# Grouped-query attention over a cache: PV three batches behind QK, K loads five ahead of V, and wo issued by GpSimd in sixteen pieces

## The chip, the core and the metric

The kernel runs on one core of a Trainium2 chip. The metric is device time in microseconds: the median of several executions. Beside it stands a profile of one execution, whose span is the time from the first to the last instruction that the profiler saw on the core.

The engines: TensorE (PE; its weight loads are shown apart as PEld), VectorE (DVE), ScalarE (ACT), GpSimd (POOL) and SyncE (SP), which here issues all DMAs. PE writes to PSUM, which has eight banks; DVE and ACT copy from there to SBUF.

## The reference

```python
B, Sq, D = 32, 4, 1024
Hq, Hkv, Sk, Dh = 32, 4, 2048, 128
q = (x @ wq).reshape(B, Sq, Hq, Dh)                  # heads to the front
k, v = k_cache, v_cache                              # each KV head serves 8 query heads
scores = einsum("bhqd,bhkd->bhqk", q, k) * Dh ** -0.5
p = softmax(scores)
o = einsum("bhqk,bhkd->bhqd", p, v)
out = o.reshape(B, Sq, Hq * Dh) @ wo
```

All is bf16. The K and V caches are 67 MB each, wq and wo 8.4 MB each. For each batch there are 4 KV heads, and 8 query heads x 4 queries = 32 rows of scores to each, so 128 rows in all, over 2048 keys.

## The kernel before

**The helper.** `Program` (L13) holds one list of operations for each engine. Each operation names the events it waits for and may name an event that it sets; `emit` (L39) turns these into semaphore waits. The order of each list is written out by hand and is the order on that engine. DMAs are in the list of the engine that issues them.

**The stream of loads** (L121 to L165). All large loads go through nine slots of SBUF (`NSLOT`), 2 MB each, in a fixed order: four loads of wq, then K of batches 0, 1, 2, then V0, K3, V1, K4 and so on (K three ahead of V), at the end V29, V30, V31, and four loads of wo, the last of which is cut in four DMAs of 512 KB. Load number n goes to slot n mod 9, so it waits until what load n - 9 brought has been used (`freed`, L131): for K that is the last transpose of the batch, for V its PV. SP issues them all. A load of K or V is 128 partitions x 4 heads x 4 KB runs; wo has runs of 2 KB. In this text a load's place is its number in the stream, counted from 0.

**The start.** x is transposed on PE (L201) and multiplied with wq into eight PSUM banks (L209); DVE and ACT copy q, transposed, to `QT_sb`.

**The loop over batches** (PE's order: L299 to L311). K has keys on partitions and must have the head dimension there, so PE transposes it: eight fills (`kt_fill`, L232) of eight transposes each, into four ring banks in turn, from which DVE (five) and ACT (three) copy to `KT_sb` (`evac`, L339). This is done two batches ahead (`AHEAD`). In iteration i PE does

- `qk(i)` (L281): 16 matmuls give the scores of 128 rows x 2048 keys, in four PSUM banks,
- `pv(i - 1)` (L262): 64 matmuls, V stationary, P^T moving, into the fourth ring bank (`ps_o`),
- the eight fills of K for batch i + 2,
- `tr_fill` (L249) x4: P is transposed by 16 matmuls against a diagonal matrix that holds 1/sum, so it is normalized by the way; two copies by DVE and two by ACT bring it to `PT_sb`, of which there is one.

Between QK and the transposes of P stand DVE's maximum over the scores (L379), its scaled negative (L380), ACT's exponential with the row sums (L408), and DVE's reciprocal (L388) and diagonal (L389). `ot_evac` (L365) copies the result of PV to `oT_sb`, for all heads and batches.

**The end.** After the loop come `pv(31)` and the output projection (`oproj`, L313): for each of 32 heads two matmuls of 512 columns, accumulated over all heads in two banks. It waits for wo and for the last `ot_evac`. DVE and ACT copy half of the result each (L398, L418), and SP stores it (L166).

**What ties the ring together.** `ring_waits` (L183) makes a fill wait for the copy out of what was in its bank four fills ago, and for the fourth bank also for the `ot_evac` of the PV that used it in between.

Of the kernel before, what the change touches and what calls it, by code (L numbers as in the profile page):

```python
# [6 lines left out]
ALU = mybir.AluOpType  # L7
# [47 lines left out]
def bass_standalone__gqa_block_cached__sampling_kernel(  # L55
# [17 lines left out]
    G = Hkv  # L73
    scale = float(Dh) ** -0.5
    NSLOT = 9
    SLOT = 8192
    NRING = 4
    KT_FILLS = 2 * G
    TR_FILLS = 4
    AHEAD = 2  # L80
    WQ_LOADS = 4
    WO_LOADS = 4
    HPL = Hq // WO_LOADS

# [5 lines left out]
    with ExitStack() as es:  # L90
# [5 lines left out]
        pp_sb = sb("pp_sb", [128, 2, Sk], BF16)  # L96
# [6 lines left out]
        P_sb = pp_sb[:, 0, :]  # L103
        PT_sb = pp_sb[:, 1, :].rearrange("p (t r) -> p t r", r=128)
        x_sb = pp_sb[:, 0, 0:D]
        xT_sb = pp_sb[:, 0, D:2 * D].rearrange("p (a b) -> p a b", b=128)
        out_sb = pp_sb[:, 1, 0:D]
# [9 lines left out]
        for n in ["x", "out"] + [f"slot{i}" for i in range(NSLOT)] + [f"wo{i}" for i in range(4)]:  # L117
            pr.sems[n] = es.enter_context(nc.semaphore(f"s_{n}"))
# [3 lines left out]
        for b in range(AHEAD + 1):  # L122
            stream.append(("k", b))
        for b in range(B):
            stream.append(("v", b))
            if b + AHEAD + 1 < B:
                stream.append(("k", b + AHEAD + 1))
# [7 lines left out]
        def slot(l):  # L135
            return slots[:, slot_of[l], :]
# [4 lines left out]
        pr.load("sp", lambda e: e.dma_start(x_sb, x_flat[:, :]), "x", "x", 16)  # L141
        for n, l in enumerate(stream):
            kind, i = l
            waits = [freed(stream[n - NSLOT])] if n >= NSLOT else []
            s, v = f"slot{n % NSLOT}", 16 * (n // NSLOT + 1)
            if kind == "wq":
                fn = lambda e, l=l, i=i: e.dma_start(slot(l), wq_v[:, i, :])  # L147
            elif kind in "kv":
                src = (k_cache if kind == "k" else v_cache)[i].rearrange("g (p t) d -> p g (t d)", p=128)
                fn = lambda e, l=l, src=src: e.dma_start(slot(l).rearrange("p (g f) -> p g f", g=G), src)  # L150
            if kind != "wo":
                pr.load("sp", fn, l, s, v, waits)
                continue
            last = i == WO_LOADS - 1
            parts = 4 if last else 1
            per = HPL // parts
            for q in range(parts):
                fn = lambda e, l=l, i=i, q=q, per=per: e.dma_start(
                    slot(l)[:, q * per * D:(q + 1) * per * D].rearrange("p (h n) -> p h n", n=D),
                    wo_v[:, i * HPL + q * per:i * HPL + (q + 1) * per, :],  # L160
                )
                if last:
                    pr.load("sp", fn, ("wo", i, q), f"wo{q}", 16, waits)
                else:
                    pr.load("sp", fn, l, s, v, waits)  # L165
# [4 lines left out]
        jobs = [("kt", b, f) for b in range(AHEAD) for f in range(KT_FILLS)]  # L170
        for i in range(B):
            if i + AHEAD < B:
                jobs += [("kt", i + AHEAD, f) for f in range(KT_FILLS)]
            jobs += [("tr", i, f) for f in range(TR_FILLS)]
        job_index = {j: n for n, j in enumerate(jobs)}
# [6 lines left out]

        def ring_waits(job):  # L183
            n = job_index[job]
            if n < NRING:
                return [("q_evac", n)]
            w = [("evac",) + jobs[n - NRING]]
            if n % NRING == 3:
                b = job[1] - AHEAD - 1 if job[0] == "kt" else job[1] - 1
                if b >= 0:  # L190
                    w.append(("ot", b))
            return w


        pr.op("pool", lambda e: e.memset(ident[:], 0.0), [], "zero")
        pr.op("pool", lambda e: e.affine_select(
            out=ident[:], in_=ident[:], compare_op=ALU.not_equal, fill=1.0, base=0,
            pattern=[[-1, 128]], channel_multiplier=1), ["zero"], "ident")
# [33 lines left out]
        def kt_fill(b, f):  # L232
            job = ("kt", b, f)
            dst = ring_bf16[job_index[job] % NRING]
            g, half = f // 2, f % 2

            def fn(e):
                for q in range(8):
                    t = half * 8 + q
                    ins = e.transpose(  # L240
                        dst[:, q * 128:(q + 1) * 128],
                        slot(("k", b))[:, (g * NKT + t) * Dh:(g * NKT + t + 1) * Dh],
                        ident[:, :],
                    )
                return ins

            pr.op("pe", fn, [("k", b)] + ring_waits(job), job)

        def tr_fill(b, f):  # L249
            job = ("tr", b, f)  # L250
            dst = ring_f32[job_index[job] % NRING]

            def fn(e):
                for q in range(4):
                    t = f * 4 + q
                    ins = e.matmul(dst[:, q * 128:(q + 1) * 128], lhsT=P_sb[:, t * 128:(t + 1) * 128],  # L256
                                   rhs=diag[:, b % 2, :], start=True, stop=True)
                return ins

            pr.op("pe", fn, [("exp", b), ("diag", b)] + ring_waits(job), job)  # L260

        def pv(b):  # L262
            def fn(e):
                v = slot(("v", b))
                for g in range(G):
                    for t in range(NKT):
                        ins = e.matmul(  # L267
                            ps_o[:, 32 * g:32 * (g + 1)],
                            lhsT=v[:, (g * NKT + t) * Dh:(g * NKT + t + 1) * Dh],
                            rhs=PT_sb[:, t, 32 * g:32 * (g + 1)],  # L270
                            start=(t == 0),
                            stop=(t == NKT - 1),
                        )
                return ins

            w = [("v", b)] + [("evac", "tr", b, f) for f in range(TR_FILLS)]
            if b > 0:
                w.append(("ot", b - 1))
            pr.op("pe", fn, w, ("pv", b))

        def qk(i):  # L281
            def fn(e):
                for c in range(Sk // 512):
                    for g in range(G):
                        ins = e.matmul(  # L285
                            ps_s[32 * g:32 * (g + 1), c * 512:(c + 1) * 512],
                            lhsT=QT_sb[:, i, REP * g:REP * (g + 1), :],
                            rhs=KT_sb[:, i % 2, g, c * 512:(c + 1) * 512],
                            start=True,
                            stop=True,  # L290
                            tile_position=(0, 32 * g),
                        )
                return ins

            w = [("evac", "kt", i, f) for f in range(KT_FILLS)]
            w += [("q_evac", j) for j in range(NB)] if i == 0 else [("exp", i - 1)]
            pr.op("pe", fn, w, ("qk", i))
# [4 lines left out]
        for i in range(B):  # L302
            qk(i)
            if i >= 1:
                pv(i - 1)
            if i + AHEAD < B:
                for f in range(KT_FILLS):
                    kt_fill(i + AHEAD, f)
            for f in range(TR_FILLS):
                tr_fill(i, f)  # L310
        pv(B - 1)  # L311

        def oproj(i, h0, n, name):  # L313
# [15 lines left out]
        for i in range(WO_LOADS):  # L329
            last = i == WO_LOADS - 1  # L330
            parts = 4 if last else 1
            for q in range(parts):
                n = HPL // parts
                pr.op("pe", oproj(i, i * HPL + q * n, n, None),
                      [("wo", i, q) if last else ("wo", i), ("ot", B - 1), ("exp", B - 1)],
                      "oproj" if last and q == parts - 1 else None)


        def evac(job):  # L339
            eng = consumer(job)  # L340
            kind, b, f = job
            n = job_index[job]
            if kind == "kt":
                g, half = f // 2, f % 2
                src = ring_bf16[n % NRING]
                dst = KT_sb[:, b % 2, g, half * 1024:(half + 1) * 1024]
                w = [job] + ([("qk", b - 2)] if b >= 2 else [])
            else:
                src = ring_f32[n % NRING]
                dst = PT_sb[:, 4 * f:4 * f + 4, :].rearrange("p a b -> p (a b)")  # L350
                w = [job] + ([("pv", b - 1)] if b > 0 else [])
# [26 lines left out]
        for i in range(B):  # L378
# [3 lines left out]
            if i >= 1:  # L382
                ot_evac(i - 1)
# [13 lines left out]
        ot_evac(B - 1)  # L397
# [73 lines left out]
```

## Time and profile before

| what | value |
|---|---|
| median of 3 runs | 388.87 us (388.68 to 389.89) |
| the profiled execution's own time | 388.88 us |
| its span | 386.9 us |
| PE, DVE, ACT busy | 77%, 63%, 51% of the span |
| GpSimd busy | 0.7 us |
| bytes read | 151.26 MB |
| mean granted TensorE clock | 0.938 |
| output projection | 64 matmuls from 368.45 to 383.32 us |

The profile's page has six parts: busy time of each engine; the span in 40 slices of 9.67 us, each digit a busy share in tenths, with the granted TensorE clock, the DMA engines' share and GB/s; DMA queues; the chain of work that ended last; groups of instructions; and DMA issues with their time to landing. Beside the page, the trace can be asked for the instructions in order of time, for who waited for whom, and for tables of stages. A time "from issue to landing" counts from the start of the issuing instruction. An SP instruction that issues a DMA can last long, since it ends only when the queue has taken the DMA.

### The profile page before, as it was taken

The page shows a single profiled execution, that of the slowest core. Times are in us where ns is not written, and L with a number is a line of the kernel's source. Part 1 is how long each engine was busy: PE and PEld are TensorE (multiplying, and loading weights), DVE is VectorE, ACT ScalarE, POOL GpSimd, SP SyncE. Part 2 cuts the span into 40 slices and gives each one's busy share as a digit, 9 for nine tenths or more (in the row PEclk, how much of TensorE's full clock was granted, in tenths as well). Part 3 has the DMA queues.
Part 4 walks back from the last instruction along what each step waited for, and adds up shares of the span by engine and source line. Part 5 has one row for each costly group of instructions (what it writes and reads, how often), then busy time and mean ns, then how long its engine had stood idle before and what let it go on. Part 6 is the DMA issues. An engine that isn't in the chain of part 4 may idle for free.

```text
span 386.9 us, 11667 instructions
## 1 busy us (share of the span) xinstructions
PE 296.0 (77%) x5448; PEld 246.8 (64%) x5448; DVE 242.4 (63%) x390; ACT 196.6 (51%) x230; POOL 0.7 (0%) x6
## 2 busy tenths in 40 slices
PE   2877787776977977878788869877777787886596
PEld 1777576665766766767667657666666677664542
DVE  0026787775777777758777757877777577774400
ACT  1024766652655565466564635666555564664300
POOL 0000000000000000000000000000000000000000
PEclk9999999998999899889898979999999898997689
DMA  8999999999999999999999999999999999999981
GB/s 327 430 412 410 407 404 407 408 408 409 406 406 409 407 409 410 406 409 407 407 409 409 405 410 410 405 409 408 407 407 407 408 409 407 409 408 359 372 327 56
DMA packets 38912, 152.26 MB, mean 393 GB/s; under 512 B 1232, under 2 KB 1232, under 8 KB 38352
## 3 DMA queue, kind: packets, MB, share of 16 engines
q1 hardware_dynamic: 38864, 151.52, 98.5%
q8 instruction: 42, 0.69, 0.7%
q14 instruction: 6, 0.05, 0.0%
HBM read 151.26 MB, written 0.26 MB: 392 GB/s over the span
## 4 chain that ended last, share of the span: by engine, by line
DMA 87%; PE 7%; ACT 2%; DVE 2%; SPq 1%; issue 0%
DMA slots<-in_k_cache_dram 87%; PE ps_s L318 4%; DVE mx L379 1%; ACT pp_sb L408 1%; PE ps_s L285 1%; ACT KT_sb L355 1%; PE ps_a L240 1%; PE ps_o L267 0%; SPq L147 0%; PE ps_o L256 0%; PE ps_a L256 0%; PE ps_b L240 0%; SPq L150 0%; PE ps_c L256 0%; PE ps_b L256 0%
## 5 line engine op out<-in xcount | busy, mean ns | idle before, releaser
L408 ACT ACTIVATE pp_sb<-ps_s,negmx 128x2048 bf16<-128x2048 f32 x32 | 62.9, 1967 | 93.1 <-DVE negmx L380 93.1
L379 DVE TENSOR_REDUCE mx<-ps_s 128x1 f32<-128x2048 f32 x32 | 73.3, 2292 | 35.3 <-PE ps_s L285 35.3
L240 PE MATMUL ps_a<-ident,slots 128*128 128x128 bf16 x512 | 43.8, 234 | 42.2 <-DMA slots<-in_k_cache_dram 41.3
L240 PEld LDWEIGHTS ps_a<-ident,slots 128*128 128x128 bf16 x512 | 33.7, 105 | 46.1 <-DMA slots<-in_k_cache_dram 44.9
L267 PEld LDWEIGHTS ps_o<-pp_sb,slots 128*128 128x128 bf16 x2048 | 53.5, 96 | 14.6 <-issue 13.7
L267 PE MATMUL ps_o<-pp_sb,slots 128*128 128x32 bf16 x2048 | 56.7, 177 | 0.8 <-ACT pp_sb L355 0.8
L355 ACT ACTIVATE KT_sb<-ps_a 128x1024 bf16<-128x1024 bf16 x32 | 32.6, 1020 | 45.6 <-PE ps_a L240 45.6
L240 PE MATMUL ps_o<-ident,slots 128*128 128x128 bf16 x512 | 42.7, 231 | 7.8 <-DVE KT_sb L353 7.8
L353 DVE COPY KT_sb<-ps_b 128x1024 bf16<-128x1024 bf16 x64 | 43.7, 683 | 5.2 <-PE ps_b L240 5.2
L353 DVE COPY KT_sb<-ps_a 128x1024 bf16<-128x1024 bf16 x32 | 22.1, 689 | 35.0 <-PE ps_a L240 35.0
L240 PE MATMUL ps_c<-ident,slots 128*128 128x128 bf16 x512 | 43.3, 233 | 0.7 <-issue 0.7
L240 PE MATMUL ps_b<-ident,slots 128*128 128x128 bf16 x512 | 43.5, 234 | 0.0
L240 PEld LDWEIGHTS ps_o<-ident,slots 128*128 128x128 bf16 x512 | 33.8, 105 | 11.4 <-DVE KT_sb L353 11.2
L240 PEld LDWEIGHTS ps_c<-ident,slots 128*128 128x128 bf16 x512 | 34.8, 105 | 1.5 <-issue 0.9
L240 PEld LDWEIGHTS ps_b<-ident,slots 128*128 128x128 bf16 x512 | 35.2, 106 | 0.4
L285 PE MATMUL ps_s<-KT_sb,QT_sb 128*32 128x512 bf16 x512 | 34.3, 389 | 0.0
L355 ACT ACTIVATE KT_sb<-ps_c 128x1024 bf16<-128x1024 bf16 x32 | 32.7, 1021 | 1.9 <-PE ps_c L240 1.9
L355 ACT ACTIVATE KT_sb<-ps_o 128x1024 bf16<-128x1024 bf16 x32 | 32.9, 1027 | 0.0
L353 DVE CAST pp_sb<-ps_a 128x512 bf16<-128x512 f32 x32 | 22.1, 692 | 12.8 <-PE ps_a L256 12.8
L256 PE MATMUL ps_o<-diag,pp_sb 128*128 128x128 bf16 x128 | 13.2, 227 | 14.7 <-ACT KT_sb L355 14.7
L353 DVE CAST pp_sb<-ps_c 128x512 bf16<-128x512 f32 x32 | 21.9, 685 | 1.9 <-PE ps_c L256 1.6
L353 DVE COPY KT_sb<-ps_c 128x1024 bf16<-128x1024 bf16 x32 | 21.9, 684 | 1.0 <-PE ps_c L240 1.0
(46 smaller groups left out, 244.7 us busy)
## 6 DMA issues: line engine op xcount, KB each, us to landing
slots<-in_k_cache_dram SPq DMA_DIRECT2D x32, 2048.0 KB, 25.0
slots<-in_v_cache_dram SPq DMA_DIRECT2D x32, 2048.0 KB, 24.2
slots<-in_wq_dram SPq DMA_DIRECT2D x4, 2048.0 KB, 14.9
slots<-in_wo_dram SPq DMA_DIRECT2D x3, 2048.0 KB, 25.6
slots<-in_wo_dram SPq DMA_DIRECT2D x4, 512.0 KB, 12.2
pp_sb<-in_x_dram SPq DMA_DIRECT2D x1, 256.0 KB, 2.7
out_dram<-pp_sb SPq DMA_DIRECT2D x1, 256.0 KB, 2.2
```

Of the source, the lines that this page charges most:

```text
L240: ins = e.transpose(dst[:, q * 128:(q + 1) * 128], slot(("k", b))[:, (g * NKT + t) * Dh:(g * NKT + t + 1) * Dh], ident[:, :],)
L256: ins = e.matmul(dst[:, q * 128:(q + 1) * 128], lhsT=P_sb[:, t * 128:(t + 1) * 128], rhs=diag[:, b % 2, :], start=True, stop=True)
L267: ins = e.matmul(ps_o[:, 32 * g:32 * (g + 1)], lhsT=v[:, (g * NKT + t) * Dh:(g * NKT + t + 1) * Dh], rhs=PT_sb[:, t, 32 * g:32 * (g + 1)], ...
L285: ins = e.matmul(ps_s[32 * g:32 * (g + 1), c * 512:(c + 1) * 512], lhsT=QT_sb[:, i, REP * g:REP * (g + 1), :], rhs=KT_sb[:, i % 2, g, c * ...
L318: ins = e.matmul(ps_s[:, c * 512:(c + 1) * 512], lhsT=oT_sb[:, h, :], rhs=w[:, h - i * HPL, c * 512:(c + 1) * 512], start=(h == 0), stop=( ...
L353: pr.op("dve", lambda e: e.tensor_copy(dst, src), w, ("evac",) + job)
L355: pr.op("act", lambda e: e.activation(dst, src, ACT.Copy), w, ("evac",) + job)
L379: pr.op("dve", lambda e, i=i: e.tensor_reduce(mx[:, i:i + 1], ps_s[:, :], AX.X, ALU.max), [("qk", i)], ("max", i))
L408: pr.op("act", lambda e, i=i: e.activation(P_sb, ps_s[:, :], ACT.Exp, bias=negmx[:, i:i + 1], scale=scale, accum_out=ssum[:, i:i + 1]), [( ...
```

## The change

Five things are changed together.

1. PV runs three batches behind QK (`LAG = 3`) in place of one, and `PT_sb` becomes `PT_buf` with four buffers. After the loop PV of batches 29, 30 and 31 are left over.
2. K is loaded five batches ahead of V (`LEAD = AHEAD + LAG`) in place of three: wq, K0 to K4, then V0, K5, V1, K6 and so on, at the end V26, K31, V27 to V31, and wo.
3. There are eight load slots for nine; the room goes to the P^T buffers.
4. All of wo is loaded in 16 pieces of 512 KB (two heads each), each with a semaphore of its own, and issued by GpSimd. Besides its slot, each piece waits until V30 has landed. The output projection waits piece by piece.
5. The ring's waits are kept by a small allocator (`take`) in place of `ring_waits`: each use of a bank waits for the copy out of the use before it, PV included. QK is recorded as four operations, with the waits on the first alone. The instructions on PE are the same.

```diff
-    NSLOT = 9
+    NSLOT = 8
...
+    LAG = 3
+    LEAD = AHEAD + LAG
+    NPT = LAG + 1
...
+    WO_PARTS = 4
+    WO_PER = HPL // WO_PARTS
...
-        pp_sb = sb("pp_sb", [128, 2, Sk], BF16)
+        P_buf = sb("P_sb", [128, Sk], BF16)
+        PT_buf = sb("PT_sb", [128, NPT, NKT, 128], BF16)
...
-        for b in range(AHEAD + 1):
+        for b in range(LEAD):
             stream.append(("k", b))
         for b in range(B):
             stream.append(("v", b))
-            if b + AHEAD + 1 < B:
-                stream.append(("k", b + AHEAD + 1))
+            if b + LEAD < B:
+                stream.append(("k", b + LEAD))
         stream += [("wo", i) for i in range(WO_LOADS)]
...
+            else:
+                for q in range(WO_PARTS):
+                    part = slot(l)[:, q * WO_PER * D:(q + 1) * WO_PER * D].rearrange("p (h n) -> p h n", n=D)
+                    h0 = i * HPL + q * WO_PER
+                    pr.load("pool", fetch(part, wo_v[:, h0:h0 + WO_PER, :]), ("wo", i, q), f"wo{i * WO_PARTS + q}", 16, waits + [("v", B - 2)])
...
+        def take(job, evac_event, bank=None):
+            if bank is None:
+                bank = turn[0] % NRING
+                turn[0] += 1
+            bank_of[job] = bank
+            before = bank_last[bank]
+            bank_last[bank] = evac_event
+            return bank, [before]
...
         def pv(b):
+            _, waits = take(("pv", b), ("ot", b), 3)
...
-                            rhs=PT_sb[:, t, 32 * g:32 * (g + 1)],
+                            rhs=PT_buf[:, b % NPT, t, 32 * g:32 * (g + 1)],
...
             qk(i)
-            if i >= 1:
-                pv(i - 1)
+            if i >= LAG:
+                pv(i - LAG)
...
-        pv(B - 1)
+        for b in range(B - LAG, B):
+            pv(b)
...
-                w = [job] + ([("pv", b - 1)] if b > 0 else [])
+                w = [job] + ([("pv", b - NPT)] if b >= NPT else [])
...
-            if i >= 1:
-                ot_evac(i - 1)
+            if i >= LAG:
+                ot_evac(i - LAG)
...
-        ot_evac(B - 1)
+        for b in range(B - LAG, B):
+            ot_evac(b)
```

More of the change, by code (lines that the diff above doesn't have):

```diff
@@ L73, in bass_standalone__gqa_block_cached__sampling_kernel @@
     G = Hkv
+    KP = 128 // G
+    KTOK = Sk // KP
+    A = KTOK // NKT
     scale = float(Dh) ** -0.5
-    NSLOT = 9
+    NSLOT = 8
     SLOT = 8192
     NRING = 4
-    KT_FILLS = 2 * G
+    KT_FILLS = KTOK // 8
     TR_FILLS = 4
     AHEAD = 2
+    LAG = 3
+    LEAD = AHEAD + LAG
+    NPT = LAG + 1
     WQ_LOADS = 4
@@ L102, in bass_standalone__gqa_block_cached__sampling_kernel @@
         rinv = sb("rinv", [128, B], F32)
[L103 to L107, printed above, removed]
+        P_sb = P_buf[:, :]
+        x_sb = P_buf[:, 0:D]
+        xT_sb = P_buf[:, D:2 * D].rearrange("p (a b) -> p a b", b=128)
+        out_sb = PT_buf[:, 0, 0:D // 128, :].rearrange("p a b -> p (a b)")
         ps_s = es.enter_context(nc.psum_tensor("ps_s", [128, Sk], F32))
@@ L116, in bass_standalone__gqa_block_cached__sampling_kernel @@
         pr.sems = {e: es.enter_context(nc.semaphore(f"s_{e}")) for e in Program.ENGINES}
-        for n in ["x", "out"] + [f"slot{i}" for i in range(NSLOT)] + [f"wo{i}" for i in range(4)]:
+        wo_sems = [f"wo{i}" for i in range(WO_LOADS * WO_PARTS)]
+        for n in ["x", "out"] + [f"slot{i}" for i in range(NSLOT)] + wo_sems:
             pr.sems[n] = es.enter_context(nc.semaphore(f"s_{n}"))
         stream = [("wq", i) for i in range(WQ_LOADS)]
-        for b in range(AHEAD + 1):
+        for b in range(LEAD):
             stream.append(("k", b))
@@ L141, in bass_standalone__gqa_block_cached__sampling_kernel, with fetch @@
         pr.load("sp", lambda e: e.dma_start(x_sb, x_flat[:, :]), "x", "x", 16)
+        pr.op("pool", lambda e: e.memset(ident[:], 0.0), [], "zero")
+        pr.op("pool", lambda e: e.affine_select(
+            out=ident[:], in_=ident[:], compare_op=ALU.not_equal, fill=1.0, base=0,
+            pattern=[[-1, 128]], channel_multiplier=1), ["zero"], "ident")
+        def fetch(dst, src):
+            return lambda e: e.dma_start(dst, src)
         for n, l in enumerate(stream):
@@ L144, in bass_standalone__gqa_block_cached__sampling_kernel @@
             waits = [freed(stream[n - NSLOT])] if n >= NSLOT else []
-            s, v = f"slot{n % NSLOT}", 16 * (n // NSLOT + 1)
+            s = f"slot{n % NSLOT}"
+            v = 16 * (n // NSLOT + 1)
             if kind == "wq":
[L147 to L165, printed above, removed]
+                pr.load("sp", fetch(slot(l), wq_v[:, i, :]), l, s, v, waits)
+            elif kind == "k":
+                src = k_cache[i].rearrange("g (p t) d -> p g (t d)", p=128)
+                pr.load("sp", fetch(slot(l).rearrange("p (g f) -> p g f", g=G), src), l, s, v, waits)
+            elif kind == "v":
+                src = v_cache[i].rearrange("g (p t) d -> p g (t d)", p=128)
+                pr.load("sp", fetch(slot(l).rearrange("p (g f) -> p g f", g=G), src), l, s, v, waits)
+            else:
[3 more added lines that the diff above has]
+                    pr.load("pool", fetch(part, wo_v[:, h0:h0 + WO_PER, :]), ("wo", i, q), f"wo{i * WO_PARTS + q}", 16, waits + [("v", B - 2)])
@@ L166, in bass_standalone__gqa_block_cached__sampling_kernel @@
         pr.op("sp", lambda e: e.dma_start(out_flat[:, :], out_sb).then_inc(pr.sems["out"], 16), ["out0", "out1"])
         pr.op("sp", lambda e: e.wait_ge(pr.sems["out"], 16))
[L170 to L175, printed above, removed]
+        bank_of = {}
@@ L177, in consumer @@
+        bank_last = {n: ("q_evac", n) for n in range(NRING)}
+        turn = [0]
+        def take(job, evac_event, bank=None):
[6 more added lines that the diff above has]
+            return bank, [before]
         def consumer(job):
@@ L181, in consumer @@
             return "dve" if f in (0, 2) else "act"
[L183 to L198, printed above, removed]
         def pe_xT(e):
@@ L233, in kt_fill @@
             job = ("kt", b, f)
-            dst = ring_bf16[job_index[job] % NRING]
-            g, half = f // 2, f % 2
+            bank, waits = take(job, ("evac",) + job)
+            dst = ring_bf16[bank]
             def fn(e):
                 for q in range(8):
-                    t = half * 8 + q
+                    t = f * 8 + q
                     ins = e.transpose(
                         dst[:, q * 128:(q + 1) * 128],
-                        slot(("k", b))[:, (g * NKT + t) * Dh:(g * NKT + t + 1) * Dh],
+                        slot(("k", b))[:, t * Dh:(t + 1) * Dh],
                         ident[:, :],
@@ L245, in fn @@
                 return ins
-            pr.op("pe", fn, [("k", b)] + ring_waits(job), job)
+            pr.op("pe", fn, [("k", b)] + waits, job)
         def tr_fill(b, f):
             job = ("tr", b, f)
-            dst = ring_f32[job_index[job] % NRING]
+            bank, waits = take(job, ("evac",) + job)
+            dst = ring_f32[bank]
             def fn(e):
@@ L258, in fn @@
                 return ins
-            pr.op("pe", fn, [("exp", b), ("diag", b)] + ring_waits(job), job)
+            pr.op("pe", fn, [("exp", b), ("diag", b)] + waits, job)
         def pv(b):
+            _, waits = take(("pv", b), ("ot", b), 3)
             def fn(e):
@@ L276, in pv, with fn @@
             w = [("v", b)] + [("evac", "tr", b, f) for f in range(TR_FILLS)]
-            if b > 0:
-                w.append(("ot", b - 1))
-            pr.op("pe", fn, w, ("pv", b))
+            pr.op("pe", fn, w + waits, ("pv", b))
         def qk(i):
-            def fn(e):
-                for c in range(Sk // 512):
+            for c in range(A):
+                def fn(e, c=c):
                     for g in range(G):
@@ L292, in fn @@
                         )
[L293 to L297, printed above, removed]
+                    return ins
+                w = []
+                if c == 0:
+                    w = [("evac", "kt", i, f) for f in range(KT_FILLS)]
+                    w += [("q_evac", j) for j in range(NB)] if i == 0 else [("exp", i - 1)]
+                pr.op("pe", fn, w, ("qk", i) if c == A - 1 else None)
         for b in range(AHEAD):
@@ L310, in bass_standalone__gqa_block_cached__sampling_kernel, with oproj @@
                 tr_fill(i, f)
-        pv(B - 1)
-        def oproj(i, h0, n, name):
+        for b in range(B - LAG, B):
+            pv(b)
+        def oproj(i, h0, n):
             def fn(e):
@@ L329, in bass_standalone__gqa_block_cached__sampling_kernel @@
         for i in range(WO_LOADS):
[L330 to L336, printed above, removed]
+            for q in range(WO_PARTS):
+                pr.op("pe", oproj(i, i * HPL + q * WO_PER, WO_PER),
+                      [("wo", i, q), ("ot", B - 1), ("exp", B - 1)],
+                      "oproj" if (i, q) == (WO_LOADS - 1, WO_PARTS - 1) else None)
         def evac(job):
@@ L341, in evac @@
             kind, b, f = job
-            n = job_index[job]
             if kind == "kt":
-                g, half = f // 2, f % 2
-                src = ring_bf16[n % NRING]
-                dst = KT_sb[:, b % 2, g, half * 1024:(half + 1) * 1024]
+                src = ring_bf16[bank_of[job]]
+                dst = KT_sb[:, b % 2, f // 2, (f % 2) * 1024:(f % 2 + 1) * 1024]
                 w = [job] + ([("qk", b - 2)] if b >= 2 else [])
             else:
-                src = ring_f32[n % NRING]
-                dst = PT_sb[:, 4 * f:4 * f + 4, :].rearrange("p a b -> p (a b)")
-                w = [job] + ([("pv", b - 1)] if b > 0 else [])
+                src = ring_f32[bank_of[job]]
+                dst = PT_buf[:, b % NPT, 4 * f:4 * f + 4, :].rearrange("p a b -> p (a b)")
+                w = [job] + ([("pv", b - NPT)] if b >= NPT else [])
             if eng == "dve":
```

## The prediction

> **What bounds the kernel now.** I read the page's 40 slices first, then its DMA issues, then the chain of waits in order of time, and last a table of stages over the last 35 us.
>
> ```profile
> PE   2877787776977977878788869877777787886596
> DMA  8999999999999999999999999999999999999981
> GB/s 327 430 412 410 407 404 407 408 408 409 406 406 409 407 409 410 406 409 407 407 409 409 405 410 410 405 409 408 407 407 407 408 409 407 409 408 359 372 327 56
> ```
>
> The DMA engines are full from the first slice to the 38th, at 405 to 410 GB/s. One load of 2 MB (2.097e6 bytes) takes 5.14 us at that rate. No compute engine comes near: PE stands at 77% of the span. So for some 350 us the order of compute matters only if it starves the loads, and a gain can only come out of the end.
>
> ```profile
> 230.35 112.13 DMA slots<-in_k_cache_dram x5
> 342.48 0.05 issue
> ...
> 366.10 1.88 PE ps_o L267 x64
> 367.98 0.02 issue
> 368.01 0.30 DVE oT_sb L368
> 368.31 0.14 issue
> 368.45 14.87 PE ps_s L318 x64
> 383.32 0.02 issue
> 383.34 0.69 DVE pp_sb L398
> ```
>
> This is the chain (start, length, what). K of batch 31 lands at 342.48. From there the end is compute: transposes, two softmax rounds of 8.95 us (max starts at 349.30 and 358.25), PV of batch 31 until 367.98, then 64 output matmuls of 14.87/64 = 0.232 us, without a wait, until 383.32. The rest to the span's 386.9 (copy, store) does not change.
>
> ```profile
> 353.00:357.00 4.00, 2.50 (x24) 1.92 (x28) 1.80 (x4) 2.06 (x4) 0.00 (x0) 0.53 0.90 312
> 357.00:360.00 3.00, 3.00 (x76) 1.94 (x68) 1.75 (x1) 0.00 (x1) 0.00 (x0) 0.50 1.02 385
> 370.00:374.00 4.00, 4.00 (x19) 1.81 (x18) 0.00 (x0) 0.00 (x0) 0.00 (x0) 0.97 1.03 382
> 374.00:378.00 4.00, 4.00 (x21) 1.80 (x19) 0.00 (x0) 0.00 (x0) 0.00 (x0) 1.00 0.54 208
> 378.00:381.00 3.00, 3.00 (x16) 1.35 (x15) 0.00 (x0) 0.00 (x0) 0.00 (x0) 1.00 0.11 41
> ```
>
> The last three columns are the granted clock, the DMA share and GB/s. The reader is to see that the loads do not end long before the compute: half of the engines' time is still used at 374 to 378. By the issue list cut to single issues, V30 (issued 329.13) lands 23.6 us later at 352.7, V31 (334.09) 25.2 later at 359.3, and the last quarter of the last wo load (369.4) 11.1 later at **380.5**. Compute ends 2.8 us after that. This 2.8 us is nearly all that a better order can win while the bytes stay the same.
>
> **The change, part by part.**
>
> *Order of loads.* K31 moves from place 64 of the stream (from 0) to place 62, so it lands 2 x 5.14 us earlier, at 332.2. V31 keeps place 67 and 359.3. Bytes, sizes and rate stay.
>
> *PV three behind.* The tail loses the K wait and gains two PVs after the last P^T. In before, the last P^T copy ends at 365.96; 10.3 earlier is 355.7. Three PVs follow, 29, 30, 31, each 1.88 plus 0.30 for its copy out and some 0.14 to hand over: 2.32 each. PV31 could start at 360.3, and its copy is done at 362.7 where V31 is there. Nothing per batch is added: the same 64 matmuls, copies and fills stand in the order, and PV still takes the bank that the batch before left.
>
> *The first batches* run without PV until i = 3 and then lag behind the loads: QK starts at 38.77, 47.64, 56.52, that is 8.88 apart, so PV0 comes at some 66.4 and ends at 68.2, while the load of place 10 (K4 now, K5 then) lands at 60.6. Cover: slots. The load of place 17 needs the slot of V0, and SP comes to place 17 at 72.73 in before, 4.5 us later. The lag melts by 10.28 - 8.88 = 1.4 us a batch. If the cover were gone, SP's loads behind it would be late too, but four to five loads (23.6 to 25.2 us from issue to landing) are still queued. Cost 0.
>
> *Eight slots for nine.* In steady state SP comes to a load some 25 us before it lands, which is when the load five places earlier lands. The slot eight places earlier was filled 15 us before that, and PE empties K in 4 us after landing (342.52 to 346.7) and V before the next K. Margin about 11 us. Cost 0; a missed slot costs at most its load, 5.14 us.
>
> *P^T with four buffers* takes away waits that cost nothing (PV's wait for P^T was 0.8 us once in the whole run).
>
> *wo on GpSimd.* SP loses seven issues, POOL gets 16 of 512 KB. The first waits for V30 (352.7); nothing else is queued on POOL. The issue cost on POOL is not in this trace. Below: SP's unblocked issues, 1.84/4 = 0.46 us for wq. Above: SP's four wo quarters behind a full queue, (15.47 - 5.61)/4 = 2.47 us. With t per issue and about 3.3 us from the last issue to landing (the 256 KB load of x alone took 2.7, and 256 KB more cost 0.65), the last piece cannot land before 352.9 + 15t + 3.3. That reaches 380.5 only at t = 1.62. POOL's queue is empty like SP's at the start, so I take the 0.46 end; any t under 1.62 gives the same sum. At 2.47 the last piece would land at 393.2.
>
> The Trainium skill speaks against this part: "DMA: Bandwidth & Descriptors", Anatomy of one DMA — SWDGE (gpsimd) path, gives a DMA from GpSimd a fixed 2.0 us plus its bytes at 436 GB/s, and its Rules for kernel authors ask for 1 MiB and more. By it a piece alone takes an estimated 3.2 us and sixteen in a row 51 us, some 23 us over the sum here; if the fixed parts overlap, it is 19 us and no bound. The trace shows no GpSimd DMA to settle it.
>
> *What the DMA engines do then.* In before V31's landing and the last wo landing are 380.5 - 359.3 = 21.2 us apart for 8.39 MB, 396 GB/s. The half of the engines that is behind is busy throughout: the dip of 353 to 357 (312 GB/s) and the half share of 374 to 378 look like the other half running dry. Starting wo at 353 instead cannot shorten the late half's work. So the last piece lands at 380.5 again, with the last four matmuls behind it: 4 x 0.232 + 0.15 = 1.1 us, end of the matmuls **381.6**.
>
> *V31 shares with wo.* From about 353.7 wo runs beside V31. V31 alone would need until 358 to 359; shared evenly its remaining 4.2 us become 8.4, landing 362.1. PV31, copy and hand-over end at 364.5, and 14.87 us of matmuls could end at 379.4. That is before 381.6, so pieces, not PE, set the end.
>
> *Clock.* In before the matmuls of 353 to 360 ran at a granted 0.50, and the first output matmuls came 0.43 us apart. At 0.43 throughout, 64 would take 27.5 us from 364.5, end 392.0 (8.7 us slower); at 0.232 nothing is lost. PE is now busy from 354 without the two 3.5 us gaps, and a paced piece keeps it busy 0.93 of 1.33 us, 70%, like the batches (77%) whose windows show mostly 1.00. I take no loss.
>
> **The sum.** Matmuls end at 381.6 for 383.32: -1.7 us. The profiled execution took 388.88 us (span 386.9 and 1.98 around it), the same as the median 388.87. Forecast 388.88 - 1.7 = **387.2 us**, 0.4% faster. About 0.3% (1.17 us) is what a measurement of this kernel tells from no change: same is 387.7 to 390.0.
>
> **Rivals.**
> 1. *Forecast*, wo's landings pace the end: 387.2 (386.4 to 387.7). Chance 0.50.
> 2. *The loads end earlier*, because the half that now runs dry is fed from the second queue; then PE sets the end, 364.5 + 14.87 = 379.4: -3.9, 385.0. For it: 0.54 of DMA share at 374. Against: each half works at its own pace, 208 GB/s for one, which is half of 408. 0.10.
> 3. *V31 is pushed back*: wo takes two shares of three, V31 lands at 353.7 + 12.6 = 366.3, the matmuls start at 368.7 and end at 383.6: 389.2, no change. 0.13.
> 4. *POOL becomes the bound*, the slower side: one mechanism, its issue time. Decides from t = 1.62; no gain from t = 1.74 (landing 382.2). At t = 2.2 landing 389.2, end 390.3, +7.0: 395.9; at 2.47 +11: 399.9. For it: an unknown price, paid 16 times in a row, with only 27 us until 380.5. Against: every row of an empty queue is under 0.6 us. 0.20.
> 5. *The change starves the stream*, that is, eight slots do not hold what the longer lead asks, in the first batches most: one or two half loads lost and not made up, +2 to +5 before the gain: 389.5 to 392. Against: 4.5 us of margin at the worst place and a deep queue. 0.07.
>
> **How the numbers follow.** Faster by over 0.3%: nearly all of 1 (0.46) and 2, 0.56. Within: 3, the rest of 1, 0.17. Slower: 4 and 5, 0.27. Likeliest is 1: 387.2. The range takes in 2 to 384.9 and 3 and 5, and of 4 what lies below 392.0; the 0.15 above that and a little below are left out.
>
> **What would show it.** Right: GB/s at 407 through slice 36; K31's transposes near 332; the last PE group waiting for DMA of wo between pieces; output matmuls ending near 381.6. Step "POOL" is wrong if POOL's issues are over 1.6 us apart and the DMA share falls below 0.9 after 358. Step "V31" is wrong if PV31 starts after 364. Step "first batches" is wrong if GB/s dips below 400 between 60 and 130 us. The forecast fails most easily on POOL's issue price, which no row here holds.

## The result, and the profile after

| | before | after |
|---|---|---|
| median | 388.75 us (388.68 to 389.89, 5 runs) | 386.51 us (386.36 to 387.55, 5 runs) |
| the profiled execution, its span | 388.88, 386.9 us | 386.50, 384.6 us |
| output matmuls | 368.45 to 383.32 us | 364.6 to 381.43 us |

The ratio is 0.9941 (95% interval 0.9923 to 0.996): 0.6% faster, where 0.4% was forecast (387.2 us). Of all runs below one, of the version with LAG = 1, lies far from the rest at 1371.3 us and is left out of its ratio.

The DMA rows of the page's 40 slices of after:

```profile
DMA  8999999999999999999999999999999999997993
GB/s 327 433 408 408 408 409 409 407 406 409 408 408 408 408 410 408 407 408 408 409 408 408 407 408 408 407 409 409 406 408 407 409 409 409 407 409 294 384 385 144
```

From slice 3 to slice 36 nothing moved: 406 to 410 GB/s, against 404 to 412 before. Slice 37 (346.1 to 355.8 us here, 348.2 to 357.9 in before) has a deeper hole than before, 294 for 359. The last slice carries more, 144 for 56, in part because it begins 2 us earlier (375.0 for 377.2). The chain of waits in order of time (start, length, what), its end:

```profile
352.48 0.59 issue
353.06 7.31 POOL slots L157 x10
360.37 0.72 POOLq L98
361.09 2.88 POOL slots L157 x4
363.97 16.37 DMA slots<-in_wo_dram
380.34 0.05 issue
380.38 1.05 PE ps_s L322 x4
381.43 0.02 issue
381.45 0.69 DVE PT_sb L398
```

In before the chain left the DMAs at 342.48 with K31 and went through 41 us of compute. Now the last thing that it comes from is the last wo piece (L157), landing at 380.34, with one piece's four matmuls (1.05 us) behind it. The same stages as those shown of before (the last three columns: granted clock, DMA share, GB/s):

```profile
353.00:357.00 4.00, 3.22 (x75) 2.98 (x73) 1.38 (x2) 1.19 (x2) 3.94 (x6) 0.50 0.82 304
357.00:360.00 3.00, 1.90 (x66) 1.71 (x62) 0.29 (x1) 0.00 (x0) 3.00 (x5) 0.50 0.99 366
370.00:374.00 4.00, 4.00 (x20) 1.82 (x19) 0.00 (x0) 0.00 (x0) 0.00 (x0) 1.00 1.02 385
374.00:378.00 4.00, 3.67 (x17) 1.40 (x16) 0.00 (x0) 0.00 (x0) 0.00 (x0) 1.00 0.91 345
378.00:381.00 3.00, 2.52 (x11) 0.81 (x10) 0.00 (x0) 0.00 (x0) 0.00 (x0) 1.00 0.12 42
```

The loads end where they ended (42 GB/s in the last stage, 41 before), and PE (the first busy time of each line) is no longer full in the last two stages: it waits for pieces. GpSimd's part, from the groups and the issue list:

```profile
L157 POOL DMA_DIRECT2D slots<-in_wo_dram x16 | 11.6, 730 | 351.6 <-DMA slots<-in_v_cache_dram 351.6
slots<-in_wo_dram POOLq DMA_DIRECT2D x16, 512.0 KB, 11.8
```

Sixteen issues of 0.73 us, all done at 364.7, 16 us before the last landing.

### The profile page after: what moved, and what is told of

It reads as the page before. It is cut to its first block, busy times and chain, and to the rows that moved or that the text cites. A ratio compares the mean times of both kernels' runs of the same rounds, so it can differ in the third digit from the quotient of the medians.

```text
span 384.6 us, 11704 instructions
## 1 busy us (share of the span) xinstructions
PE 293.0 (76%) x5446; PEld 241.3 (63%) x5448; DVE 241.5 (63%) x390; ACT 196.3 (51%) x230; POOL 12.3 (3%) x22
## 4 chain that ended last, share of the span: by engine, by line
DMA 78%; ACT 9%; DVE 5%; PE 4%; POOL 3%; SPq 1%; issue 0%; POOLq 0%
DMA slots<-in_k_cache_dram 68%; DMA slots<-in_v_cache_dram 6%; ACT KT_sb L354 5%; DMA slots<-in_wo_dram 4%; DVE mx L378 4%; ACT P_sb L408 4%; POOL slots L157 3%; PE ps_s L286 2%; PE ps_o L257 1%; SPq L157 1%; DVE negmx L379 0%; PE ps_a L240 0%; PE ps_s L322 0%; PE ps_o L240 0%; PE ps_c L240 0%
## 5 line engine op out<-in xcount | busy, mean ns | idle before, releaser
L408 ACT ACTIVATE P_sb<-ps_s,negmx 128x2048 bf16<-128x2048 f32 x32 | 63.0, 1967 | 92.8 <-DVE negmx L379 92.8
L240 PE MATMUL ps_a<-ident,slots 128*128 128x128 bf16 x512 | 42.0, 228 | 38.3 <-DMA slots<-in_k_cache_dram 34.8
L270 PEld LDWEIGHTS ps_o<-PT_sb,slots 128*128 128x128 bf16 x2048 | 53.7, 96 | 16.7 <-issue 15.8
L270 PE MATMUL ps_o<-PT_sb,slots 128*128 128x32 bf16 x2048 | 57.0, 177 | 3.7 <-issue 2.0
L240 PE MATMUL ps_b<-ident,slots 128*128 128x128 bf16 x512 | 41.8, 228 | 0.0
L240 PEld LDWEIGHTS ps_b<-ident,slots 128*128 128x128 bf16 x512 | 33.4, 103 | 1.3
L352 DVE CAST PT_sb<-ps_a 128x512 bf16<-128x512 f32 x32 | 22.1, 692 | 12.8 <-PE ps_a L257 12.8
L257 PE MATMUL ps_o<-diag,P_sb 128*128 128x128 bf16 x128 | 13.2, 227 | 14.4 <-ACT KT_sb L354 14.4
L157 POOL DMA_DIRECT2D slots<-in_wo_dram x16 | 11.6, 730 | 351.6 <-DMA slots<-in_v_cache_dram 351.6
L352 DVE CAST PT_sb<-ps_c 128x512 bf16<-128x512 f32 x32 | 21.9, 683 | 1.1 <-PE ps_c L257 1.0
```

What stands on the lines that cost most here:

```text
L157: return lambda e: e.dma_start(dst, src)
L240: ins = e.transpose(dst[:, q * 128:(q + 1) * 128], slot(("k", b))[:, t * Dh:(t + 1) * Dh], ident[:, :],)
L270: ins = e.matmul(ps_o[:, 32 * g:32 * (g + 1)], lhsT=v[:, (g * NKT + t) * Dh:(g * NKT + t + 1) * Dh], rhs=PT_buf[:, b % NPT, t, 32 * g:32 * ...
L352: pr.op("dve", lambda e: e.tensor_copy(dst, src), w, ("evac",) + job)
L408: pr.op("act", lambda e, i=i: e.activation(P_sb, ps_s[:, :], ACT.Exp, bias=negmx[:, i:i + 1], scale=scale, accum_out=ssum[:, i:i + 1]), [( ...
```

## The experiments

The theory after the result, A: the end is the last wo landing plus one piece's matmuls; the lag of PV only takes compute out of the way of that. Rivals: B, the gain is GpSimd's queue, which feeds wo past SP's full one; C, the lag alone makes the gain and how wo comes does not matter. All runs are five rounds beside the kernel before, in three sessions (the first four versions, the next three, the last four); times are medians, ratios are to the kernel before in the same session, whose medians were 389.0, 389.1 and 389.4 us.

**The lag alone undone.**

```diff
-    LAG = 3
+    LAG = 1
```

> The changed kernel with LAG = 1: PV one batch behind QK and K three ahead of V, as before, with wo still on GpSimd in 16 pieces. Theory A (the end is the last wo landing plus one piece's matmuls, and the lag of PV takes compute out of the way of that): K of batch 31 is back at place 64, its chain ends as before with the first output matmul near 368.4 us and the last near 383.3, so 388.4 to 389.0 us. Theory B (the gain is GpSimd's queue, which feeds wo past the full queue of SP): 386.5 us, as with the whole change.

Measured 388.43 us, ratio 0.9989 (0.9972 to 1.0005): no gain left. Its chain ends as that of before, 64 matmuls without a wait:

```profile
368.58 14.75 PE ps_s L322 x64
383.33 0.02 issue
```

So B is out: GpSimd's queue by itself moves nothing.

**GpSimd undone.**

```diff
-                    pr.load("pool", fetch(part, ...), ..., 16, waits + [("v", B - 2)])
+                    pr.load("sp", fetch(part, ...), ..., 16, waits)
```

> The changed kernel with the 16 pieces of wo issued by SP behind V31 and without the wait for V30. Theory A: the half of the DMA engines that is late has the same bytes in the same order, the last piece lands at 380.0 to 380.8 us and the matmuls end near 381.5: 386.2 to 387.0 us. Theory B: without GpSimd's queue the gain is gone: 388.7 us.

Measured 386.21 us, ratio 0.9927 (0.9914 to 0.9941), the same as the whole change. PE in order of time:

```profile
364.12 7.93 PE L322 MATMUL ps_s<-slots,oT_sb 128*128 128x512 bf16 x36 [0.48 <-DVE oT_sb L367]
...
380.11 1.04 PE L322 MATMUL ps_s<-slots,oT_sb 128*128 128x512 bf16 x4 [0.24 <-DMA slots<-in_wo_dram]
```

The matmuls start half a microsecond earlier and end 0.3 us earlier, paced by the pieces. The hole of slice 37 was filled for the most part (353 GB/s from 353 to 357, against 304 with GpSimd), and that moved the last landing by 0.3 us only.

**Large pieces.**

```diff
-    WO_PARTS = 4
+    WO_PARTS = 1
```

> The changed kernel with wo in four loads of 2 MB on GpSimd, so that 16 matmuls hang on the last landing for 4. Theory A: the last load lands near 380.3 us as now, 16 x 0.232 = 3.7 us of matmuls behind it in place of 1.05, end near 384.1: 389.0 to 389.4 us. Theory C (the lag of PV alone makes the gain, the pieces do nothing): 386.5 us.

Measured 389.27 us, ratio 1.0003 (0.9991 to 1.0016). The end of its chain:

```profile
356.21 24.41 DMA slots<-in_wo_dram
380.62 0.04 issue
380.67 3.64 PE ps_s L322 x16
```

The landing is nearly where it was (380.62 for 380.34); 3.64 us hang on it for 1.05, and the whole gain is gone. C is out: it matters how wo comes. But this is not the lag alone. The kernel before already had its last load of wo in quarters of 512 KB, and lag 3 with that loading was not run. An estimate from the traces: the third load landed at 375.33 in before, and its 16 matmuls and the 16 of the last load, 3.64 us for each 16, would end at 382.7, which is 0.6 us before 383.32, where the whole change gains 1.89. By that the cut of the first three loads is worth something too, but this is not shown.

**wo issued later.**

```diff
-                    ... waits + [("v", B - 2)])
+                    ... waits + [("v", B - 1)])
```

> The changed kernel with GpSimd's first piece waiting for V31 in place of V30. Theory A: V31 lands at 357.5 us, GpSimd issues 0.6 later, and from issue to the first bytes some 2 us pass in which the late half of the DMA engines has nothing: the last landing moves from 380.3 to 382.3 to 383.3 and the end with it, 388.5 to 389.5 us. Theory C: PE starts the output projection only at 364.6 us anyway, so nothing changes: 386.5 us.

Measured 390.65 us, ratio 1.004 (1.0025 to 1.0054): the direction of A, but more than I had put. The table by stages and the end of the chain:

```profile
356.00:360.00 4.00, 3.23 (x109) 2.94 (x105) 0.46 (x2) 0.00 (x0) 1.76 (x3) 0.50 0.20 57
...
384.79 0.05 issue
384.84 1.05 PE ps_s L322 x4
```

With the engines empty the first piece took 4.0 us from its issue at 358.24 to its landing, and the last landed 4.4 us later than with the wait for V30; I had put 2 to 3.

**One PV less of lag.**

```diff
-    LAG = 3
+    LAG = 2
```

> The changed kernel with LAG = 2: K31 at place 63, two PVs left over. Theory A: against the whole change the chain from K31 loses one load (5.14 us) and saves one PV (2.32), so the first output matmul moves from 364.6 to 367.4 us; 64 of them, the first ones at half clock, end at 382.3 to 383.3, just behind the landings (380.3 plus 1.05): 387.4 to 388.4 us, between the change and before. Theory B (GpSimd's queue makes the gain): 386.5 us.

Measured 387.51 us, ratio 0.9951 (0.9931 to 0.9971): between. The matmuls start at 366.67, do not wait for a piece, and take 16.06 us.

**wo issued earlier.**

```diff
-                    ... waits + [("v", B - 2)])
+                    ... waits + [("v", B - 4)])
```

> The changed kernel with GpSimd's first piece waiting for V28 (342.3 us) in place of V30, so that wo is issued while three loads of V are in SP's queue. Theory A with even sharing of each DMA engine, as the prediction had it: wo's bytes go between those of V29, V30 and V31, V31 lands at 366 to 370 in place of 357.5 us, PV31 and 64 matmuls follow, 388.7 to 392 us. Rival: a DMA engine works off what SP queued first (as V31's landing at 357.5, 5.0 after V30, looks): V31 lands near 357.5, and 386.5 us.

Measured 391.61 us, ratio 1.006 (1.004 to 1.008). Who PE waited for from 362 to 372 us (total, times, longest), and the chain's end:

```profile
PE ps_o L270 <- DMA slots<-in_v_cache_dram: 6.7, 1, 6.7
```

```profile
368.94 1.90 PE ps_o L270 x64
370.85 0.02 issue
370.87 0.30 DVE oT_sb L367
371.17 0.14 issue
371.31 15.84 PE ps_s L322 x64
```

V31 landed at 368.9 in place of 357.5: the two queues share the DMA engines once both have bytes there. The last wo piece (issued at 353.9, 26.4 us to landing) landed at 380.3 all the same. So issuing wo ten microseconds earlier brings its end no nearer; it only pushes V31 back.

**32 pieces on SP.**

```diff
-    WO_PARTS = 4
+    WO_PARTS = 8
...
+                    pr.load("sp", fetch(part, ...), ..., 16, waits)
```

> The changed kernel with wo issued by SP, without the wait for V30, in 32 pieces of 256 KB (one head each). Theory A: the last landing stays near 380.1 us, two matmuls hang on it for four, 0.46 us less: 385.6 to 386.0 us against 386.2 for 16 pieces on SP, the best of the versions. Theory C (pieces do nothing): 386.2 us. If the smaller pieces cost the DMA engines time, the last landing is later and it is 386.3 us or more.

Measured 387.13 us (385.74 to 387.77), ratio 0.9937 (0.9914 to 0.996): a miss. In its profiled execution (386.4 us) the matmuls start at 365.84, 1.7 us later than with 16 pieces on SP, since PE stood still for 1.98 us in PV30. PE waits for no piece until the last three, and the last matmuls of two take 0.62 us for the 0.46 I had put. The last landing is 380.78, 0.72 later than with 16 pieces on SP, but V31 was already 0.82 later (358.40 for 357.58), so in this execution it is not the small pieces that made it late. Why its runs lie 2 us apart the one profile does not tell.

**Half of wo.** Only the first two loads of wo stay, and the projection uses them twice.

```diff
-        stream += [("wo", i) for i in range(WO_LOADS)]
+        stream += [("wo", i) for i in range(WO_LOADS // 2)]
...
-                w = slot(("wo", i)).rearrange("p (h n) -> p h n", n=D)
+                w = slot(("wo", i % 2)).rearrange("p (h n) -> p h n", n=D)
```

> The changed kernel with only the first half of wo loaded (eight pieces, 4.2 MB), which the output projection uses twice; the matmuls stay. It tells how far compute stands behind the loads. Theory A: the last landing comes some 10.6 us earlier, at 369.7, and nothing paces the matmuls any more; they start at 364.6 and take 14.8 to 16.1 us as in the runs where PE did not wait, end 379.4 to 380.7: 384.5 to 385.8 us, so compute is only 1 to 2 us behind the loads. If compute had much room, it would be 382 us or less.

Measured 385.53 us, ratio 0.9888 (0.9857 to 0.9919). No piece paces PE any more, and its matmuls still run until 379.12 in the profiled execution, which is the fastest of the six (384.15 us). By the medians of its session the gain over the change (386.24 us, run again below) is 0.7 us, by the profile 2.3 us (379.12 for 381.43): about 1 to 2 us is all that a faster stream of wo could bring while compute stays as it is.

**A shorter PV.** The trace has 16 landing events for each load; I take them as one for each DMA engine. Eight of them are late: from 352 to 354 us, when only the late parts of V31 were left, the packets took 50.3% of the 16 engines' time. The landing of three loads of after, part by part in order of time, in microseconds behind the first part:

```
place 4    0.0 0.0 0.1 0.1 0.2 0.2 0.3 0.3 0.4 0.4 0.4 0.4 0.4 0.5 0.6 2.0
place 18   0.0 0.1 0.2 0.3 0.4 0.6 0.8 1.0 1.5 1.8 1.8 1.8 1.9 1.9 3.5 3.5
place 67   0.0 0.1 0.2 0.2 0.4 0.6 1.5 3.0 7.7 7.9 7.9 7.9 8.0 8.0 8.1 8.1
```

In between, one part after the other falls back by some 1.5 us, each time one of the 43 instruction fetches of 16 KB has run (the queue q8 of the page). Forty of them ran before V31 landed, five rounds of the same eight parts, and five times 1.6 us are the 8 us of place 67. From the sixth on the fetches' own durations repeat every eight as well: 1.03, 1.03, 1.09, 1.08, 1.07, 1.11, 1.11, 1.09 us and again. The experiment leaves out three quarters of PV, and so 3072 instructions and their fetches, at the same bytes of data:

```diff
-                    for t in range(NKT):
+                    for t in range(NKT // 4):
```

> The changed kernel with PV over 4 of its 16 key blocks (3072 instructions fewer on PE, the bytes loaded are the same; the result of PV is partial). Theory I (new): the late half of the DMA engines is late because the 43 instruction fetches of 16 KB go to those eight engines in turn, some 1.6 us each; with 11 to 12 fetches fewer they are 2.2 to 2.4 us less late, the last wo piece lands near 378.0 and 384.0 to 384.5 us follow, since compute ends earlier too. Rival: that half is late for another reason, the last landing stays at 380.3: 386.3 to 386.7 us.

Measured 384.10 us (384.02 to 384.33), ratio 0.986 (0.9829 to 0.9892). Its instruction queue, and the end of its chain:

```profile
q8 instruction: 31, 0.51, 0.5%
```

```profile
362.81 15.07 DMA slots<-in_wo_dram
377.88 0.05 issue
377.93 1.05 PE ps_s L322 x4
```

Twelve fetches fewer (after has 43), and the last piece lands 2.46 us earlier, at 377.88 for 380.34, with 378.0 expected. PE waits for each of the last ten pieces, so it is the landing that moved the end. A rival is that less work on PE speeds up all loads. It is not so: the first part of V31 landed no sooner (349.82 for 349.35), only the late half did (its last part at 356.32 for 357.47).

**Eight pieces of 256 KB at the end.** wo on SP, and only the last load in eight pieces of one head.

```diff
+                per = WO_PER if i < WO_LOADS - 1 else 1
+                for q in range(HPL // per):
...
+                    pr.load("sp", fetch(part, ...), ..., 16, waits)
```

> Wo issued by SP in twelve pieces of 512 KB and, for the last load, eight of 256 KB, without the wait for V30. Theory A: two matmuls hang on the last landing for four: 0.46 us under wo on SP in 16 pieces, 385.7 us. If the small pieces cost the DMA engines what the 32 pieces did, it is 386.5 us or more.

Measured 385.87 us (385.62 to 387.2), ratio 0.9912 (0.9881 to 0.9943).

**The change again**, beside these three:

> The changed kernel once more, beside the three: 386.5 us, and 380.3 us for the last landing.

Measured 386.24 us, ratio 0.9914 (0.9885 to 0.9943), last landing 380.05. The version with eight small pieces at the end is 0.4 us under it by medians; their ratios are the same within their intervals, so it is not shown to be faster.

## Why the prediction was right, point by point

- *Order of loads.* K31's transposes start at 332.15; 332.2 was forecast. Right.
- *PV three behind.* PV29 starts at 355.43, 0.3 earlier than the chain gave; PV30 follows 2.34 later, against 2.32 (PV31 does not, see V31 below). Right, and needed: with LAG = 1 the time is that of before, with LAG = 2 between.
- *First batches and eight slots at no cost.* GB/s stays at 406 to 410 from slice 3 to slice 36 (the forecast read the row of before as 405 to 410 from the first slice to the 38th; it has 404 to 412 from slice 3 to slice 36, and 327, 359 and 372 in slices 1, 37 and 38). And SP reaches place 17 at 72.72, as before at 72.73. Place 16 was issued 1.8 us late (64.07 for 62.28), without a trace in the DMA rows. Right.
- *POOL.* 0.73 us an issue against the 0.46 I took and the 1.62 from which it would count. Right by its bound. The fixed 2.0 us that the Trainium skill ("DMA: Bandwidth & Descriptors", Anatomy of one DMA) gives a GpSimd DMA does not add up over a row of DMAs: after the second, pieces land 1.2 to 1.5 us apart while others are in flight, where the page's fixed part and bytes make an estimated 3.2 us each. Alone, in the wait for V31, the first piece took 4.0 us on empty engines, 0.8 more than that estimate, and there the wait cost the whole gain and more.
- *The half that is late is busy throughout.* The last landing, forecast 380.5, came at 380.34, and at 380.06 to 380.3 where wo was fed sooner by SP or 10 us earlier by GpSimd. Right; rival 2 falls with it.
- *V31 shares with wo.* **Wrong here.** V31 lands at 357.5, 5.0 after V30, not at 362.1. The first packets of wo moved at 354.6, 1.6 us after GpSimd's first issue and 2.9 us before V31 landed, yet V31 kept its rate: from 354.6 to 356.5 its packets took 50.6% of the 16 engines' time, as much as from 352 to 354 without wo (50.3%), and wo's took the other 49.3%. So V31 went on on the late half and wo moved on the half that had run dry. That the queues can share an engine's time is right, as the wait for V28 shows (V31 at 368.9), and something like rival 3 is what happens if wo is issued earlier; why they did not share here is open. The start of the matmuls, 364.6 for 364.5 forecast, was right by luck, two errors that cancel: PE stood still for 2.0 us in the midst of PV30, which nothing in my working had:

```profile
357.77 1.60 PE L270 MATMUL ps_o<-PT_sb,slots 128*128 128x32 bf16 x54 [0.47 <-DVE oT_sb L367]
361.38 0.45 PE L270 MATMUL ps_o<-PT_sb,slots 128*128 128x32 bf16 x10 [2.01 <-issue]
362.31 1.86 PE L270 MATMUL ps_o<-PT_sb,slots 128*128 128x32 bf16 x64 [0.47 <-DVE oT_sb L367]
```

- *Clock.* The granted clock was 0.50 to the middle of 365 to 370 and 1.00 from 370 on, paced pieces included. So it stayed low through the three PVs, though I had counted on PE being busy enough from 354 on. The first output matmuls ran at half clock as in before; I had counted 14.87 us for all, and 14.75 to 16.06 are what unpaced runs took. From 364.6 that ends at 379.35 to 380.66, 0.8 to 2.1 us before 381.43, for the 2.2 us that I had between 379.4 and 381.6. No loss, as forecast, but with less room.
- *The sum.* Matmuls end 1.89 us earlier, against 1.7. The other half microsecond of 2.4 between the profiled executions lies behind them: from the end of the last copy to the issue of the store 0.34 us passed in before (384.03 to 384.37) and 0.04 now, and the store itself landed 2.0 us after its issue for 2.2. No run here was made to find out why.

## What to carry to other kernels

When the loads run full from start to end, look at which of the two ends last, the loads or the compute on what landed early, and by how much: here 2.8 us was all that an order could win at the same bytes and instructions, and it took both a deeper lag (compute off the end) and small last pieces (less work on the last landing) to get two thirds of it: with LAG = 1, or with loads of 2 MB, nothing was left. Which queue issued the last loads did not matter; when they were issued did: too early pushes back what compute waits for (V31 at 368.9 for 357.5), too late leaves the DMA engines empty (57 GB/s from 356 to 360).

## What the runs showed of the hardware that I had not expected

- Instruction fetches cost data bandwidth where it is the bound. 43 fetches of 16 KB (0.70 MB beside 151) fell on eight of the sixteen engines in turn, each set its engine back some 1.5 us, and when V31 landed these eight were 8 us behind the others. Leaving out 12 fetches brought the end of the loads 2.46 us forward. The Trainium skill's "Runtime: NRT & Kernel Launch", Terms, has instruction memory refilled in blocks of 16 KB, which fits the size of these packets. The same page, in Instruction fetch mechanics, calls the cost of crossing such a block "mostly hidden"; here the measurement says otherwise. Fewer instructions on PE could thus be worth time in a kernel whose PE is 76% busy and not the bound.
- PE stood still for 2.0 to 2.3 us in PV30, always after 54 of the 64 matmuls, in the change, its repetition, the 2 MB pieces, the wait for V28 and the 32 pieces on SP, and not in the other versions. The trace speaks for a wait for an instruction fetch. In these five runs a fetch began 0.3 to 0.4 us before PE stopped (359.02 in the change, where PE stopped at 359.37), and PE went on 2.35 to 2.6 us after the fetch had begun. In the versions with the wait for V31, with 16 or 20 pieces on SP and with half of wo, the same fetch began 2.3 us or more before PE came to this place, and PE did not stop there for more than 0.3 us. Why the fetch began late in the five was not found out.
- Whether SP or GpSimd issued the 16 pieces, the time was the same at the end (386.21 and 386.51 us), though each issue takes 0.73 us of GpSimd's own time.
